# Transposes of the combining weights spread over the experts' stage, the last ten behind its last product; first weight conversions begun two places earlier

## The chip, the core and the metric

The kernel runs on one core of a Trainium2 chip, in one launch. A core has a matrix engine (TensorE, PE in the rows; its weight loads are shown as PEld), a vector engine (VectorE, DVE), a scalar engine (ScalarE, ACT), a general one (GpSimd, POOL) and a queue that issues transfers (SyncE, SP). Each works through its own list of instructions in order, and they wait for each other by semaphores. PE writes its results to a small memory, PSUM, from which ACT or DVE copy them to SBUF, the large on-chip memory. The metric is the device time of one execution in microseconds (us).

## The reference

Three layers follow each other, all in float32. Attention of 8 batches x 8 heads between 512 tokens and 32 state rows, in both directions; a mixture of experts that mixes all 4,608 tokens into 32 slots, runs 8 experts of 4 slots each, and mixes the slots back; and a gated layer over all tokens. Cut to what matters here:

```python
# x: 4608 x 512, phi: 512 x 32, w1: 8 x 512 x 1024, w2: 8 x 1024 x 512
logits = x @ phi
d = softmax(logits, over tokens)
slot_input = (d.T @ x).reshape(8, 4, 512)
for e in range(8):
    slot_out[e] = np.maximum(slot_input[e] @ w1[e], 0.0) @ w2[e]
c = softmax(logits, over slots)            # the combining weights, 4608 x 32
x = c @ slot_out
g = x @ w_gate                             # 512 x 1536
out = (g * sigmoid(g) * (x @ w_val)) @ w_out
```

## The kernel before, in words

The attention comes first (to about 90 us); its order is a written list of short names. Then the experts' stage, and then the last stage, which takes the last 330 us. In the last stage the product with `slot_out` is never made for itself: `slot_out` (the tile `ST`) is multiplied into the gate and value weights once (`fold`, line 842), and the blocks of tokens then multiply their combining weights with these folded weights (line 1169), gate the result and multiply it with the output weights (line 1219).

For that the combining weights must stand transposed, 32 slots by 4,608 tokens, in the tile `cstack`. `c_calc` (line 614) makes them in three generators: `c1` for the first 16 tiles of 128 tokens, `c2` for the next 16 and `c3` for the last 2. Each takes the softmax over slots (DVE, ACT, POOL), splits it into two float16 parts (tile `cc`, on POOL), and then, in groups of eight tiles, has PE transpose them into a PSUM tile (line 628) and ACT copy that to `cstack` (line 629). There are 34 such transposes in five groups: 8, 8, 8, 8 and 2.

The experts run as two groups `g` of four. For a group, `expert_1` takes the first layer's products (line 645), one call step for each of eight 1 MB weight loads; `expert_r` applies scale and ReLU on ACT or DVE (lines 655, 657); `expert_h` transposes the result on PE (line 664) and copies it back (line 666); `expert_2` takes the second layer's products in eight steps `k` (line 676); `expert_o` copies the two halves of the result out of PSUM (`so`, line 692: for group 1 the first half on ACT and the second on DVE), turns them with products against a selection matrix (line 694), and writes or adds them to `ST` (lines 703, 705). After group 1 the last stage starts: ST's maximum is taken (line 973), spread over all rows by a product (line 755), and `fold` multiplies `ST` with the converted weights.

Weights of the last stage arrive as 64-bit numbers whose halves are turned into float32 by `to32` (line 715): one ACT conversion (line 725), then a shift (729), a merge (732) and a second merge (736) on DVE. Before the last stage this is done for two blocks of gate and value weights, `pg` (`prep_w0`), and for the first block of output weights, `pw` (`prep_wo0`). Behind the conversion `pw` takes a maximum (826), spreads it on PE (755), derives a scale on DVE (763 to 829), and writes scaled float16 parts on ACT (833) and DVE (837).

The order of all this is written out by hand: `some(gen, n)` lets a generator take its next n pieces, `run(gen)` all that are left, and every engine gets its instructions in the order in which these calls come. Loads are issued by SP in one list; each waits until its buffer of a ring of 17 is free. `heat(n)` issues n filler products whose result nobody uses.

Of the kernel before, what the change touches and what calls it, by code (L numbers as in the profile page):

```python
# [8 lines left out]
F16 = mybir.dt.float16  # L9
# [20 lines left out]
G0 = 10  # L30
G2 = 0
G1 = 5
CC = 0
NRM = 0, 1
ATD = 1
PA, PB, PC = 0, 0, 0
# [2 lines left out]
HA, HB = 7, 5  # L39
H2 = 0  # L40
H7 = 0
HP_ = 0, 1
LEAD, RATE = 7, 21
CR = 1.0
CN = 2.0
# [39 lines left out]
def attn_moe_glu_kernel(  # L85
# [14 lines left out]
    pe, act, dve, pool = nc.tensor, nc.scalar, nc.vector, nc.gpsimd  # L100
# [31 lines left out]
    def psum(i, shape, dt=F32):  # L132
        return ps[-1].tile(shape, dt, tag=f"p{i}", name=f"p{i}")
# [3 lines left out]
    def psmall(shape, dt=F32):  # L137
        scnt[0] += 1
        i = scnt[0] % (3 - len(ps))
        return ps[-1].tile(shape, dt, tag=f"s{i}", name=f"s{i}")  # L140
# [446 lines left out]
    def heat(n, i=None, src=None):  # L587
        src = ident if src is None else src
        p = pbig([128, 128]) if i is None else psum(i, [128, 128])
        for _ in range(n):  # L590
            pe.matmul(out=p, lhsT=src, rhs=src, start=True, stop=True)
# [17 lines left out]
        (pool, dve)[PA].tensor_tensor(out=dst, in0=dst, in1=bc(r, NSL), op=ALU.mult)  # L609
        yield 1.0  # L610

    CT = []

    def c_calc(t0, n):
        c = wk.tile([128, n, NSL], F32, tag=("sp", "so", "edn")[t0 // 16], bufs=1 + t0 // 32, name="cc")
        yield from slot_softmax(Lg[:, t0:t0 + n, :], n, c)
        cc = wk.tile([128, n, 4, NSL], F16, tag=("stn", "C", "edn")[t0 // 16], bufs=1 + t0 // 32, name="cc16")
        for i in range(2):
            pool.tensor_copy(out=cc[:, :, i, :], in_=c) if i >= PB else act.copy(out=cc[:, :, i, :], in_=c)
        yield 1.0  # L620
        for i in range(2):
            (pool, dve)[i < PC].tensor_tensor(out=cc[:, :, 2 + i, :], in0=c, in1=cc[:, :, i, :], op=ALU.subtract)
        yield 1.0
        for u in range(0, n, 8):
            k = min(8, n - u)
            p = psmall([128, 8, 128], F16)
            for i in range(k):
                pe.transpose(p[:, i, :], cc[:, u + i, :, :].rearrange("p a s -> p (a s)"), CT[1])
            (dve.tensor_copy if (u // 8) % 2 < CC else act.copy)(out=CT[0][:, t0 + u:t0 + u + k, :], in_=p[:, :k, :])
            yield 1.0  # L630

    hT, SO, HP = {}, {}, {}

# [26 lines left out]
    def expert_h(g, i):  # L660
        q = psmall([128, 4, 128])
        h = hS.pop(i)
        for k in range(4):
            pe.transpose(q[:, k, :], h[:, k * 128:(k + 1) * 128], ident)
        t = exq[0][:, 1024 + 512 * i:1536 + 512 * i].rearrange("p (k n) -> p k n", k=4)
        (act.copy, dve.tensor_copy)[i and not g](out=t, in_=q)  # L666
        hT[g, i] = t

    def expert_2(g, lo, hi):
        if lo == 0:  # L670
            SO[g] = [psum(i, [128, 256]) for i in ((2, 0), (2, 1))[g]]
        for k in range(lo, hi):
            for i in range(2):
                u = got.pop(("w2", g, k, i)) if g and k == 7 else got["w2", g, k][:, :, 256 * i:256 * i + 256]
                for j in range(4):
                    pe.matmul(out=SO[g][i][32 * j:32 * j + 32, :], lhsT=hT[g, k // 4][:, k % 4, 32 * j:32 * j + 32],  # L676
                              rhs=u[:, j, :], start=(k == 0), stop=(k == 7))
                if g and k == 7:
                    done()
                    if i == 0:  # L680
                        heat(H7, 0)
            if not (g and k == 7):
                got.pop(("w2", g, k))
                done()
# [12 lines left out]
    def expert_o(g):  # L697
        for i in range(2):
            expert_p(g, i)
            if g:  # L700
                heat(HP_[i], 0)
        if g == 0:
            act.copy(out=ST[:, 0:4, :], in_=OP[g])
        else:
            dve.tensor_tensor(out=ST[:, 0:4, :], in0=OP[g], in1=ST[:, 0:4, :], op=ALU.add)
# [312 lines left out]
    def run(*gens):  # L1018
        for gen in gens:
            for _ in gen:  # L1020
                pass

    def some(gen, n):
        for _ in range(n):
            if next(gen, None) is None:
                return
# [28 lines left out]
    with tc.manual_schedule():  # L1055
# [45 lines left out]
        CT.append(wk.tile([128, 128], F16, tag="gh", name="id16"))  # L1101
        dve.tensor_copy(out=CT[1], in_=ident)
        c1, c2, c3 = c_calc(0, 16), c_calc(16, 16), c_calc(32, 2)
        pw, pg = prep_wo0(), prep_w0()
# [6 lines left out]
        expert_h(0, 0)  # L1111
        expert_r(0, 1)
        some(c2, 4 - C2)
        expert_2(0, 0, 3)
        expert_h(0, 1)
        some(c3, 4)
        expert_2(0, 3, 8)
        some(pg, 10)
        expert_1(1, 0, 1)
        expert_o(0)  # L1120
        warm = sm.tile([128, 1], F32, tag="warm", bufs=1, name="warm")
        act.activation(out=warm, in_=va, func=AF.Silu)
        run(c1)
        expert_1(1, 1, 2)
        run(c2)
        expert_1(1, 2, 4)
        expert_r(1, 0)
        run(c3)
        some(pg, 1)
        expert_1(1, 4, 5)  # L1130
        run(pg)
# [6 lines left out]
        some(pw, 4)  # L1138
        expert_2(1, 0, 3)
        expert_h(1, 1)  # L1140
        expert_2(1, 3, 4)
        run(pw)
        expert_2(1, 4, 8)
        expert_o(1)
        ps1.close()
        ps.append(ctx.enter_context(tc.tile_pool(name="ps2", bufs=1, space=PSUM)))
# [199 lines left out]
```

## Time and profile before

| | us |
|---|---|
| runs before: median (lowest to highest of 3) | 466.17 (465.02 to 468.76) |
| the profiled execution | 466.66 |
| its span, from the first to the last instruction | 464.9 |
| PE busy in the span | 441.1 |
| DVE, ACT, POOL busy | 300.4, 245.8, 180.9 |
| mean granted clock of PE, share of full speed | 0.996 |

The profile is of one execution, by hardware. A row of a timeline merges instructions of one line that follow each other: start, busy time, engine, line, operation, the tile written and the tile read, number of records; in brackets the idle time of the engine just before and who ended it. A float32 product shows as two records. Line numbers are those of the kernel before.

### The profile page before, as it was taken

The numbers are of one execution on the slowest core, as the hardware profiler recorded it, in microseconds if no ns is written. First come the engines' busy times: TensorE is split into PE (matmuls) and PEld (weight loads), VectorE is DVE, ScalarE is ACT, GpSimd is POOL, SyncE is SP. The second block draws the span as 40 slices with busy tenths as digits, with TensorE's granted clock in tenths as the row PEclk, the third lists the DMA queues.
The fourth block names the chain that finished last, engine by engine and source line by source line (L and its number), as shares of the span: only waits on it lengthen the run. The fifth ranks groups of instructions, "written<-read, shape, count | busy, mean of one in ns | idle before, by whom it ended". The sixth has DMA issues, their size and how long they took to land.

```text
span 464.9 us, 9476 instructions
## 1 busy us (share of the span) xinstructions
PE 441.1 (95%) x3723; PEld 244.9 (53%) x3723; DVE 300.4 (65%) x610; ACT 245.8 (53%) x439; POOL 180.9 (39%) x160
## 2 busy tenths in 40 slices
PE   8789998999988999898999999999999999999997
PEld 6477676544453455454555555555555555555553
DVE  3877988467667786968999878544333334345454
ACT  2678877427348797774655644433344433344440
POOL 0113221072017565644756453333333333333331
PEclk9999999999999899999999999999999999999999
DMA  8999999999999203300000000000011112211224
GB/s 313 421 420 413 413 419 419 390 363 421 419 418 421 87 5 126 155 12 1 1 13 0 7 7 1 13 0 1 1 47 45 47 45 57 80 47 45 90 92 180
DMA packets 19436, 75.04 MB, mean 161 GB/s; under 512 B 5440, under 2 KB 6080, under 8 KB 12608
## 3 DMA queue, kind: packets, MB, share of 16 engines
q1 hardware_dynamic: 19392, 74.45, 40.2%
q8 instruction: 29, 0.48, 0.4%
q14 instruction: 15, 0.12, 0.1%
HBM read 64.87 MB, written 8.91 MB: 159 GB/s over the span
## 4 chain that ended last, share of the span: by engine, by line
PE 70%; DMA 9%; DVE 7%; issue 5%; POOL 5%; ACT 3%; SPq 0%; POOLq 0%; DVEq 0%; ACTq 0%
PE p L1219 44%; PE p L1169 7%; DMA u<-in_wgv_dram 4%; DMA u<-in_xn_dram 4%; PE p L676 3%; POOL hl L1183 3%; PE p L645 3%; PE p L270 2%; POOL u L723 2%; PE p L315 2%; DVE osb L1233 1%; PE s L370 1%; DMA stN<-in_stn_dram 1%; PE s L443 1%; DVE sh L1174 1%
## 5 line engine op out<-in xcount | busy, mean ns | idle before, releaser
L1219 PE MATMUL p<-wo,hl 128*128 128x512 f16 x1014 | 238.2, 381 | 1.8 <-DVE osb L1233 1.7
L1183 POOL TENSOR_TENSOR hl<-sh,hl 128x512 f16<-128x512 f32 x102 | 126.4, 1240 | 191.9 <-ACT hl L1182 188.5
L1219 PEld LDWEIGHTS <-hl 128*128 128x128 f16 x1218 | 118.4, 98 | 123.9 <-issue 4.4
L1174 DVE SCALAR_TENSOR_TENSOR sh<-p,segk,sh 128x512 f32<-128x512 f32 x102 | 76.2, 747 | 85.0 <-ACT sh L1170 83.7
L1170 ACT ACTIVATE sh<-p,sg 128x512 f32<-128x512 f32 x85 | 58.4, 687 | 128.6 <-PE p L1169 128.6
L1182 ACT CAST hl<-sh 128x512 f16<-128x512 f32 x102 | 62.4, 612 | 12.7 <-DVE sh L1174 12.6
L1233 DVE SCALAR_TENSOR_TENSOR osb<-p,segm,osb 128x512 f32<-128x512 f32 x67 | 49.9, 746 | 22.4 <-PE p L1219 22.2
L1219 PE MATMUL p<-bqm,hl 128*128 128x512 f16 x204 | 49.6, 379 | 0.0
L1169 PE MATMUL p<-cstack,gvs 128*128 128x256 f16 x272 | 41.5, 274 | 0.8 <-DVE sh L1174 0.5
L1169 PEld LDWEIGHTS <-gvs 128*128 128x128 f16 x272 | 26.7, 99 | 19.2 <-issue 2.2
L357 POOL TENSOR_TENSOR a<-a,r 128x1024 f32<-128x1024 f32 x7 | 13.4, 1915 | 56.3 <-DVE r L353 17.2
L732 DVE SCALAR_TENSOR_TENSOR u<-u 128x512 uint32<-128x512 uint32 (+1 forms) x33 | 26.4, 809 | 13.4 <-POOL u L723 13.2
L723 POOL TENSOR_SCALAR u<-u 128x512 uint32<-128x512 uint8 x30 | 26.5, 884 | 2.5
L1231 ACT ACTIVATE osb<-p,segk 128x512 f32<-128x512 f32 x28 | 19.2, 692 | 5.2 <-PE p L1219 5.2
L1169 PE MATMUL p<-cstack,gv 128*128 128x256 f16 x136 | 20.4, 273 | 0.0
L736 DVE SCALAR_TENSOR_TENSOR gvf<-gvf,u 128x512 uint32<-128x512 uint32 (+1 forms) x22 | 19.9, 913 | 0.2
L315 PE MATMUL p<-cs,atA 128*128 128x128 f32 x128 | 17.9, 277 | 1.8 <-DVE atA L280 0.5
L1169 PEld LDWEIGHTS <-gv 128*128 128x128 f16 x136 | 13.3, 98 | 8.8
L310 ACT ACTIVATE atA<-atA,nm 128x512 f32<-128x512 f32 x16 | 10.7, 718 | 12.1 <-PE p L315 12.1
L315 PEld LDWEIGHTS p<-cs,atA 128*128 128x128 f32 x128 | 14.3, 140 | 3.6 <-DVE atA L280 1.0
L676 PE MATMUL p<-u,exq 128*32 128x256 f32 x256 | 14.8, 380 | 0.7 <-ACT exq L666 0.7
L725 ACT ACTIVATE gvf<-u 128x512 f32<-128x512 f32 (+1 forms) x22 | 14.8, 722 | 0.0
(214 smaller groups left out, 451.3 us busy)
## 6 DMA issues: line engine op xcount, KB each, us to landing
u<-in_w_dram SPq DMA_DIRECT2D x23, 1024.0 KB, 13.8
u<-in_wgv_dram SPq DMA_DIRECT2D x12, 1024.0 KB, 17.4
u<-in_xn_dram SPq DMA_DIRECT2D x8, 1040.0 KB, 17.9
out_dram<-osb SPq DMA_DIRECT2D x15, 512.0 KB, 2.8
early<-in_w_dram SPq DMA_DIRECT2D x14, 512.0 KB, 9.1
u<-in_wo_dram SPq DMA_DIRECT2D x6, 1024.0 KB, 17.8
u<-in_xt_dram SPq DMA_DIRECT2D x3, 1024.0 KB, 7.3
early<-in_w_dram SPq DMA_DIRECT2D x1, 1024.0 KB, 9.8
```

Of the source, the lines that this page charges most:

```text
L315: pe.transpose(p[:, j, q * 128:(q + 1) * 128], stsA[:, q, j * 128:(j + 1) * 128], ident)
L676: pe.matmul(out=SO[g][i][32 * j:32 * j + 32, :], lhsT=hT[g, k // 4][:, k % 4, 32 * j:32 * j + 32], rhs=u[:, j, :], start=(k == 0), stop=(k ...
L723: pool.tensor_scalar(out=lo[:, c], in0=byte[:, c], scalar1=2.0 ** -5, scalar2=-31.0 / 64, op0=ALU.mult, op1=ALU.add)
L732: dve.scalar_tensor_tensor(out=lo[:, c], in0=hi[:, c], scalar=0x80000000, in1=lo[:, c], op0=ALU.bitwise_and, op1=ALU.bitwise_or)
L736: dve.scalar_tensor_tensor(out=tu[:, c], in0=tu[:, c], scalar=3, in1=lo[:, c], op0=ALU.logical_shift_left, op1=ALU.bitwise_or)
L1169: pe.matmul(out=p[v][:, 256 * i:256 * i + 256], lhsT=GV[2 * q + i][v], rhs=rhs, start=True, stop=True)
L1170: act.activation(out=sh[:, 0, :], in_=p[0], func=AF.Silu, scale=sgs[q])
L1174: dve.scalar_tensor_tensor(out=sh[:, 1, :], in0=p[1], scalar=(kap0[0] if k == 0 else seg_scale(*seg)[0][q]), in1=sh[:, 0, :], op0=ALU.mult ...
L1182: act.copy(out=t[:, 0, :], in_=sh[:, 1, :])
L1183: pool.tensor_tensor(out=t[:, 1, :], in0=sh[:, 1, :], in1=t[:, 0, :], op=ALU.subtract)
L1219: pe.matmul(out=accs[x], lhsT=t[:, u // 2, c], rhs=WO[2 * q + j][:, u % 2, :], start=first and u == 0 and j == 0, stop=last and (j, u) == ...
L1233: dve.scalar_tensor_tensor(out=o, in0=accs[i], scalar=rsc, in1=o, op0=ALU.mult, op1=ALU.add)
```

## The change

`c_calc` gives its last part, one group's transposes and copy, to a new function `c_move`, and keeps its `cc` tile where that can find it. The calls are moved:

- the first two groups (of `c1`) go from behind group 0's `expert_o` to places between the steps of its `expert_2`;
- the third group (the first of `c2`) keeps its place;
- the fourth group and the last two transposes go behind the last products of group 1's `expert_o`, in one PSUM tile of the tag `p0`; the one filler product that stood there is gone;
- the first three pieces of `pg` (one ACT conversion, the shift and the first merge on DVE) go ahead of group 0's `expert_2`;
- the rest of `pw` goes from behind step 3 to behind step 5 of group 1's `expert_2`.

```diff
     def c_calc(t0, n):
...
+        CCS[t0] = cc
...
         for u in range(0, n, 8):
-            k = min(8, n - u)
-            p = psmall([128, 8, 128], F16)
-            for i in range(k):
-                pe.transpose(p[:, i, :], cc[:, u + i, :, :].rearrange("p a s -> p (a s)"), CT[1])
-            (dve.tensor_copy if (u // 8) % 2 < CC else act.copy)(out=CT[0][:, t0 + u:t0 + u + k, :], in_=p[:, :k, :])
+            c_move(t0, u, min(8, n - u), psmall([128, 8, 128], F16))
             yield 1.0
+
+    def c_move(t0, u, k, p):
+        for i in range(k):
+            pe.transpose(p[:, i, :], CCS[t0][:, u + i, :, :].rearrange("p a s -> p (a s)"), CT[1])
+        act.copy(out=CT[0][:, t0 + u:t0 + u + k, :], in_=p[:, :k, :])
...
     def expert_o(g):
         for i in range(2):
             expert_p(g, i)
-            if g:
-                heat(HP_[i], 0)
+        if g:
+            p = psum(0, [128, 16, 128], F16)
+            c_move(16, 8, 8, p[:, 0:8, :])
+            c_move(32, 0, 2, p[:, 8:10, :])
...
         some(c2, 4 - C2)
+        some(pg, 3)
         expert_2(0, 0, 3)
         expert_h(0, 1)
+        some(c1, 1)
         some(c3, 4)
-        expert_2(0, 3, 8)
-        some(pg, 10)
+        expert_2(0, 3, 6)
+        some(c1, 1)
+        expert_2(0, 6, 8)
+        some(pg, 7)
         expert_1(1, 0, 1)
         expert_o(0)
...
-        run(c1)
         expert_1(1, 1, 2)
-        run(c2)
+        some(c2, 1)
         expert_1(1, 2, 4)
         expert_r(1, 0)
-        run(c3)
         some(pg, 1)
...
-        expert_2(1, 3, 4)
+        expert_2(1, 3, 6)
         run(pw)
-        expert_2(1, 4, 8)
+        expert_2(1, 6, 8)
         expert_o(1)
```

What this does to the engines' lists is seen at three places. In the changed file the transposes and their copy are lines 629 and 630, the fold is line 849, and other lines of the last stage are two to four higher than before.

The first place is PE's list around the end of the experts' stage (`so`: the copied result, `p_1952`: the PSUM tile of the last transposes, `cc_1605` and `cc_1675`: the parts of `c2` and `c3`, `gvf` and `ST`: the fold's operands). Before:

```order
L694 MATMUL s_1957<-cs,so 128x32 [waits Activation_49]
...
L694 MATMUL s_1957<-cs,so 128x32 [waits DVE_49]
...
L591 MATMUL p_1967<-cs 128x128
L847 MATMUL p_1985<-gvf,ST 32x128 [waits DVE_49,PE_49]
L847 MATMUL p_1985<-gvf,ST 32x128 x7
L755 MATMUL s_1994<-cs,mst 128x128 [waits DVE_49]
```

And in the change, where the pair of rows `cc_1605` stands eight times:

```order
L694 MATMUL s_1943<-cs,so 128x32 [waits Activation_49]
...
L694 MATMUL s_1943<-cs,so 128x32 [waits DVE_49]
...
L629 LDWEIGHTS cc_1605
L629 MATMUL p_1952<-id_1522,cc_1605 128x128
...
L629 LDWEIGHTS cc_1675 [waits Pool_49]
L629 MATMUL p_1952<-id_1522,cc_1675 128x128 [waits Activation_49]
L629 MATMUL p_1952<-id_1522,cc_1675 128x128
L849 MATMUL p_1981<-gvf,ST 32x128 [waits DVE_49,Activation_49]
L849 MATMUL p_1981<-gvf,ST 32x128 x7
L757 MATMUL s_1990<-cs,mst 128x128 [waits DVE_49]
```

The filler is gone, and ten transposes stand between the L694 products and the fold. Two waits for ACT are new: in the built program the ninth transpose waits for the count that ACT reaches with the copy of the first eight, and the fold's first product for the count that it reaches with the copy of the last two.

The second place is ACT's list from the first experts' result on (`gvf` and `wof`: converted weights, `cstack`: the copies of transposes, `so`: copies of results). Before:

```order
L666 COPY exq<-s_1591 128x512 [waits PE_49]
L601 ACTIVATE cc<-cc 128x64 [waits DVE_49]
L725 ACTIVATE gvf<-u 128x1024 [waits DMAHW7_49,DMAHW5_49]
L725 ACTIVATE gvf<-u 128x1024 [waits DMAHW6_49,DMAHW0_49]
L692 COPY so<-p_1610 128x256 [waits PE_49]
L692 COPY so<-p_1611 128x256 [waits PE_49]
```

In the change:

```order
L666 COPY exq<-s_1591 128x512 [waits PE_49]
L727 ACTIVATE gvf<-u 128x1024 [waits DMAHW7_49,DMAHW5_49]
L630 COPY cstack<-s_1653 128x1024 [waits DMAHW5_49,PE_49]
L599 ACTIVATE cc<-cc 128x64 [waits DVE_49]
L630 COPY cstack<-s_1710 128x1024 [waits PE_49]
L727 ACTIVATE gvf<-u 128x1024 [waits DMAHW6_49,DMAHW0_49]
L692 COPY so<-p_1615 128x256 [waits PE_49]
L692 COPY so<-p_1616 128x256 [waits PE_49]
```

The first conversion moved up, and the second now stands behind two copies to `cstack`. On DVE the shift and the first merge of the same weights likewise moved up, from behind the `c3` softmax to ahead of the copy of line 666.

The third place is PE's list in group 1's second layer (`p_1864` and `p_1850`: the first half of the result, `mxw`: the maximum of the output weights). Before:

```order
L676 MATMUL p_1864<-u,exq 32x256 [waits DMAHW5_49]
...
L755 MATMUL s_1904<-cs,mxw 128x128 [waits DVE_49,PE_49]
...
L676 MATMUL p_1864<-u,exq 32x256 [waits DMAHW6_49,Activation_49]
...
L676 MATMUL p_1864<-u,exq 32x256 [waits DMAHW7_49]
...
L676 MATMUL p_1864<-u,exq 32x256 [waits DMAHW0_49]
...
L676 MATMUL p_1864<-u,exq 32x256 [waits DMAHW1_49]
```

In the change (these are the rows that begin a step; the rest of each step is left out in both):

```order
L676 MATMUL p_1850<-u,exq 32x256 [waits DMAHW5_49]
...
L676 MATMUL p_1850<-u,exq 32x256 [waits DMAHW6_49,Activation_49]
...
L676 MATMUL p_1850<-u,exq 32x256 [waits DMAHW7_49]
...
L757 MATMUL s_1906<-cs,mxw 128x128 [waits DVE_49,PE_49]
...
L676 MATMUL p_1850<-u,exq 32x256 [waits DMAHW0_49]
...
L676 MATMUL p_1850<-u,exq 32x256 [waits DMAHW1_49]
```

The product that spreads the maximum moved from behind step 3 to behind step 5, so two steps are left behind it where four were. On ACT and DVE the work that hangs on it (lines 833 and 837 of the kernel before) still stands ahead of the copies `so`.

## Rows read from the trace of the kernel before

**Rows 1.** The page, engines: busy us, share of the span, instructions.

```profile
PE 441.1 (95%) x3723; PEld 244.9 (53%) x3723; DVE 300.4 (65%) x610; ACT 245.8 (53%) x439; POOL 180.9 (39%) x160
```

**Rows 2.** Chain of waits, 107 to 130 us: start us, us, what.

```profile
107.04 1.02 PE s L694 x8
...
112.34 1.85 PE p L645 x16
114.19 0.22 PE s L628 x2
...
115.41 0.64 PE s L755 x4
...
123.66 0.42 PE s L755 x2
124.08 3.20 PE p L676 x56
...
127.74 0.04 issue
127.79 1.09 PE s L694 x8
...
129.34 0.64 PE p L847 x16
```

**Rows 3.** Timeline of PE, 107 to 152 us.

```profile
107.89 1.12 PE L628 MATMUL s<-id,cc 128*128 128x128 f16 x16
...
110.82 0.61 PE L628 MATMUL s<-id,cc 128*128 128x128 f16 x8 [0.81 <-ACT cstack L629]
...
136.19 2.76 PE L1219 MATMUL p<-wo,hl 128*128 128x512 f16 x12
...
151.29 1.34 PE L847 MATMUL s<-gvf,ST 128*32 128x128 f32 x28 [2.25 <-DVE gvf L736]
```

**Rows 4.** Timeline of ACT, 103 to 127 us.

```profile
103.45 2.32 ACT L725 ACTIVATE gvf<-u 128x1024 f32<-128x1024 f32 x2
...
114.91 0.37 ACT L629 COPY cstack<-s 128x256 f16<-128x256 f16 x1
...
125.21 1.34 ACT L833 ACTIVATE wo<-wof,wsc 128x512 f16<-128x512 f32 x2 [1.92 <-DVE wsc L829]
```

**Rows 5.** Groups of ACT's instructions, 107 to 113 us: busy us, mean ns.

```profile
L629 ACT COPY cstack<-s 128x1024 f16<-128x1024 f16 x4 | 3.7, 1018 | 0.0
```

**Rows 6.** Timeline of DVE, 101 to 143 us.

```profile
101.77 0.69 DVE L666 COPY exq<-s 128x512 f32<-128x512 f32 x1 [2.14 <-PE s L664]
...
104.72 0.71 DVE L729 TENSOR_SCALAR u<-u 128x1024 uint32<-128x1024 uint32 x1
105.46 1.23 DVE L732 SCALAR_TENSOR_TENSOR u<-u 128x1024 uint32<-128x1024 uint32 x1
...
125.96 1.42 DVE L837 SCALAR_TENSOR_TENSOR wo<-wof,wsc,wo 128x512 f16<-128x512 f32 x2 [0.79 <-ACT wo L833]
127.74 0.42 DVE L692 COPY so<-p 128x256 f32<-128x256 f32 x1 [0.36 <-PE p L676]
...
142.56 0.69 DVE L732 SCALAR_TENSOR_TENSOR u<-u 128x512 uint32<-128x512 uint32 x1 [1.67 <-POOL u L723]
```

**Rows 7.** SP's issue of the last half-load of `w2`; and its us to landing.

```profile
108.06 0.33 SPq L174 DMA_DIRECT2D u<-in_w_dram  x1
...
u<-in_w_dram SPq DMA_DIRECT2D x1, 512.0 KB, 17.1
```

**Rows 8.** Stretches: us, busy PE, PEld, DVE, ACT, POOL, granted clock, DMA share, GB/s.

```profile
12.50:16.50 4.00, 1.88 (x40) 0.60 (x42) 3.45 (x9) 2.53 (x4) 1.39 (x1) 1.00 1.00 418
108.00:112.00 4.00, 2.88 (x38) 1.81 (x36) 3.84 (x5) 3.88 (x6) 0.47 (x2) 1.00 1.01 420
152.00:156.00 4.00, 4.00 (x23) 1.78 (x23) 2.33 (x4) 2.05 (x5) 2.66 (x3) 0.57 0.38 158
153.00:153.50 0.50, 0.50 (x3) 0.23 (x2) 0.00 (x0) 0.50 (x2) 0.50 (x1) 0.50 0.74 311
```

More of the change, by code (lines that the diff above doesn't have):

```diff
@@ L32 @@
 G1 = 5
-CC = 0
 NRM = 0, 1
@@ L41 @@
 H7 = 0
-HP_ = 0, 1
 LEAD, RATE = 7, 21
@@ L610, in slot_softmax @@
         yield 1.0
-    CT = []
+    CT, CCS = [], {}
     def c_calc(t0, n):
```

## The prediction

> **What bounds the kernel now.** I began with the page: TensorE (PE) is busy nearly all the span [rows 1], so what counts is time in which PE waits or is made to wait. The change touches one stretch, from about 98 to 131 us, where the two groups of four experts are computed and the first weights of the last stage are folded. So the next view is the chain of waits through that stretch [rows 2]. The reader is to see two things. From 108.06 (107.04 + 1.02) to 112.34 the chain goes through the transposes of the combining weights: 4.28 us in which PE does 32 of the 34 transposes and only one block of expert products. And from 123.66 on it runs over PE, ACT and PE again: the last products, the copies of their result, and the fold at 129.34, from which the whole last stage hangs.
>
> The timelines say what happens inside. On PE [rows 3] sixteen transposes take 1.05 us (107.89 to the next start at 108.94), and the third group of eight starts only after 0.81 us of waiting for ACT's copy of an earlier group. On ACT one such copy takes 1.02 us [rows 5]. On DVE [rows 6] the row at 101.77 has 2.14 us of idle time ahead of it, which is where the early conversions go. A load of the second layer's weights lands 17 us after its issue [rows 7]. The granted clock is 1.00 of full speed (2.4 GHz) in the stretch with the transposes [rows 8].
>
> **The change, part by part.**
>
> *Transposes spread.* The first two groups of eight now stand between the first group's second-layer products, before 108.06: they cost what they cost before, 1.05 us, and their copies on ACT have products to hide behind. So the L694 products end at 108.06 + 1.05 = 109.11. Then one block of products (half of the 1.85 us that sixteen take [rows 2], 0.93) and one group of eight (0.53) follow, and the row that began at 112.34 begins at 109.11 + 0.93 + 0.53 = 110.57, 1.77 us sooner. The two transposes at 114.19 (0.22) are gone from there too. PE is 1.99 us ahead at the row of 115.41.
>
> *First conversions begun early.* One ACT conversion, and a shift and a merge on DVE, are moved ahead. On DVE they need 0.71 + 1.23 = 1.94 us [rows 6], and the idle time before the 101.77 copy is 2.14: nothing on the path. If that cover were short (GpSimd works beside it) the copy would be late by at most one merge, 1.23, and PE needs it one group of transposes (0.53) and one step (0.91) after its start: 0 to 0.5 us, I take 0. The second ACT conversion (1.16, half of 2.32 [rows 4]) now stands behind a cstack copy and ahead of the copies that release L694; it ends about 107.6, and PE is in a block of products until 108.1: 0. The buffers of the second-layer weights come free up to 1.05 us later, and SP, whose order is unchanged, issues the next loads later by that; with 17 us between issue and landing the landing times stay. The last half-load, issued at 108.06, lands at 125.2 [rows 7], and its use falls at 125.3: 0, with 0.4 as its bound.
>
> *Scaling of the first output weights (L755, L833, L837) moved two steps back.* Before, L755 stood behind step 3 (counted from 0) of the eight, at 123.66. Now it stands behind step 5: 123.66 - 1.99 + 2 x 0.91 (0.91 is 16/56 of the 3.20 us row) = 123.50. Almost the same time, but PE now has only two steps left behind it: the products end at 123.50 + 0.42 + 1.83 = 125.75. What hangs on L755 takes as long as before: DVE's L837 ended 127.38 - 123.66 = 3.72 us after it [rows 6], so now at 127.22; ACT's L833 ended 2.89 us after it [rows 4], now at 126.39. Both stand ahead of the copies `so` on their engines. So DVE's copy of the second half, which waited 0.36 us for PE before, now waits for DVE's own L837: it runs from 127.25 to 127.67, and after a hand-over of 0.04 [rows 2] the second half of L694 (half of 1.09) ends at 128.26. Before it ended at 128.88. Of 1.99 us, 0.62 are left; 1.4 us became a wait for ACT and DVE.
>
> *The last ten transposes.* They follow L694 directly. The filler that stood there lay beside DVE's addition, so its removal gives nothing. If only PE counted, the ten would cost 0.61 + 0.22 and the fold would begin at 129.1. But the order with its waits shows more: the ninth transpose waits for ACT's copy of the first eight, out of the same tile; and the fold waits for ACT's copy of the last two. That makes a round trip: eight transposes (0.61) to 128.87, ACT's copy (1.02) to 129.93, two transposes (0.22) to 130.19, ACT's copy (0.37) to 130.60, fold at 130.64, each with a hand-over of 0.04. Queued behind the waiting fold on PE are L755 for ST's maximum and the second half of the fold, and for these wait ACT's `gt` and the scale of everything after.
>
> *Sum.* 130.64 - 129.34 = **+1.30 us** at the start of the last stage. That stage is tied to its own start (its first conversion on DVE, at 142.56, waits for POOL and for no load [rows 6]), so the difference stays. The profiled execution took 466.66 us; one like it takes 467.96. The median of the runs shown lies 0.49 below the profiled one: **467.5 us**. Bounds of the sum: from +0.8 (copies that overlap with the drain of the transposes, PE's start 0.4 better) to +2.2 (late DVE copy and late half-load together).
>
> *A rule against the change.* [Rows 8] show 108 to 112, with 32 transposes in it, at a granted clock of 1.00, 2.4 GHz. The Trainium skill (TensorE: Matmul & The Clock Gate, Part 4: PE-mode transpose) says that transposes do not count as activity of PE for its clock in the way products do. By that rule the ten transposes hold the clock less than the removed filler did, and the time would be that of rival 2. The row does not bear it out, and does not refute it, as products stood around the transposes.
>
> **Rivals.**
>
> 1. *The fold does not wait for the copies*: they are done in time, or the waits are for something long past. Then the fold starts at 129.1, 0.25 us earlier than before: 465.9 us, not slower. It decides from the point where both copies are through when DVE has added ST. For it: ACT has nothing else to do then. Against: a copy's own 1.02 us, which no idle ACT makes shorter. Chance 0.15.
>
> 2. *The clock falls.* PE sat idle for 2.25 us until 151.29 [rows 3], and from 152 to 156 the mean granted clock was 0.57, with 0.50, which is 1.2 GHz, inside [rows 8]. By the sum above PE is idle about 1.1, 0.4, 1.1 and 0.4 us between 125.75 and 130.64, with 1.9 us of short work between. A fall would slow the fold and what follows it. The fall of 152 to 156 cost 0.43 x 4 = 1.7 us; here some of the work is ACT's and DVE's, so I put it at 1.5 (an estimate from that row). Against: in 12.5 to 16.5 PE was busy for no more than 1.88 us and the clock stayed at 1.00. 1.3 + 1.5 = 2.8: 469.0 us. Chance 0.17.
>
> 3. *The later fall goes away.* If the shift by 1.3 us spares the stretch at 152 to 156, PE gets 1.7 us back: 1.3 - 1.7 = -0.4, 465.8 us. For it: the fall stands behind one idle time of PE, and where that lies in the span moves. Against: nothing in the change works on it, and its own length stays. Chance 0.10.
>
> 4. *The scaling chain is no wait*, because L755 runs sooner. Then the fold starts up to 1.4 us earlier than in my sum, and the spread pays for the round trip: 466.1. It would need L755 at 122.1; PE's place in its own queue sets it (the chain goes through PE there). Chance 0.05.
>
> **How the numbers follow.** Forecast 0.53, rivals 0.15, 0.17, 0.10, 0.05. The likeliest case gives 467.5, with its own bounds 467.0 to 468.4. The range takes in the rivals on both sides: 465.4 to 469.5. One per cent, about what a measurement of this kernel can tell from no change, is 4.7 us; no case reaches it alone. Faster by over 1% would need rivals 3 and 4 and more: 0.03. Slower by over 1% needs a fall of the clock that lasts longer than the one seen: 0.06. The rest, 0.91, is within 1%.
>
> **What would show it.** Right: PE's second half of the L694 products waits for DVE's `so` copy behind L837; the last two transposes wait about 1 us for ACT's cstack copy; the fold waits for the second one; the first L1219 row starts 1.3 us later than at 136.19 [rows 3]; no stall of PE at the remaining transposes near 110. Wrong: a fold that starts before 129.5, a first L1219 row before 136.0, a granted clock below 1.00 between 126 and 136, or a new wait of PE between 98 and 108 for DVE's copy or for a load.

## The result, and the profile after

| | before | after |
|---|---|---|
| median of the runs | 467.65 us (11 runs, 465.02 to 469.46) | 470.62 us (11 runs, 468.74 to 472.38) |
| profiled execution, span | 466.66, 464.9 us | 470.62, 468.9 us |

The change makes the kernel slower: ratio 1.0067, 95% interval 1.0039 to 1.0096, which is 3.0 us by the medians. That lies within one per cent, as forecast, but above the range: 467.5 was predicted, and 465.4 to 469.5 were given.

The part of the program ahead of the experts' stage is the same in all kernels here, and its length differs from one profiled execution to the next: the first L645 product of the stage starts between 89.9 and 92.2 us. So in all that follows, places are counted from that product, 90.01 us before and 91.36 after. The difference of the two is 1.35.

Here is PE in the changed kernel, from the scaling's L757 (L755 before) to the first product of the output weights, L1223 (L1219 before). Each line has the start, the duration (both us), engine and line, operation and tiles, shape and count; in brackets the idle time ahead of it and what ended that.

```profile
124.71 0.49 PE L757 MATMUL s<-cs,mxw 128*128 128x128 f32 x2
125.13 1.99 PE L676 MATMUL p<-u,exq 128*32 128x256 f32 x32
127.97 0.63 PE L694 MATMUL s<-cs,so 128*128 128x32 f32 x4 [0.84 <-ACT so L692]
128.88 0.63 PE L694 MATMUL s<-cs,so 128*128 128x32 f32 x4 [0.28 <-DVE so L692]
129.35 0.61 PE L629 MATMUL p<-id,cc 128*128 128x128 f16 x8
131.06 0.27 PE L629 MATMUL p<-id,cc 128*128 128x128 f16 x2 [1.10 <-ACT cstack L630]
131.79 1.08 PE L849 MATMUL p<-gvf,ST 128*32 128x128 f32 x16 [0.46 <-ACT cstack L630]
...
140.50 0.82 PE L1223 MATMUL p<-wo,hl 128*128 128x512 f16 x3
```

First the four waits: 0.84, 0.28, 1.10 and 0.46 us, 2.68 us in all. In the kernel before, PE had a single one on its way to the fold:

```profile
129.34 0.64 PE L847 MATMUL p<-gvf,ST 128*32 128x128 f32 x16 [0.17 <-DVE ST L705]
```

Less 1.35, the fold starts at 130.44 on the scale of before: 1.10 us later than at 129.34, against 1.30 in the sum. Then the fold's own duration: its sixteen products take 1.08 us and not the 0.64 of [rows 2]. And then the last line: 140.50 - 1.35 = 139.15, 2.96 us later than the 136.19 of [rows 3]. So 1.86 us more are lost between the fold and the first product of the output weights.

Why that is, the granted clock tells. This is a table of stretches of the changed kernel, with the columns of [rows 8]; the clock is the third number from the end.

```profile
108.00:112.00 4.00, 4.00 (x48) 1.97 (x36) 3.84 (x4) 2.91 (x5) 1.09 (x5) 1.00 1.02 422
128.00:132.00 4.00, 2.16 (x22) 1.75 (x26) 1.44 (x4) 1.39 (x2) 0.00 (x0) 0.93 1.01 420
131.50:132.00 0.50, 0.21 (x4) 0.20 (x8) 0.00 (x0) 0.24 (x1) 0.00 (x0) 0.50 1.10 459
132.00:136.00 4.00, 3.57 (x43) 2.23 (x36) 1.48 (x7) 0.34 (x2) 0.00 (x0) 0.50 1.01 416
137.50:138.00 0.50, 0.50 (x4) 0.38 (x4) 0.45 (x2) 0.00 (x0) 0.00 (x0) 0.50 1.02 426
138.50:139.00 0.50, 0.26 (x3) 0.09 (x1) 0.00 (x0) 0.50 (x2) 0.00 (x0) 1.00 1.02 426
```

Through the last waits ahead of the fold the clock goes from 1.00 to 0.50, which is 1.2 GHz, and it is back at 1.00, 2.4 GHz, by 138.5. That is the fall that rival 2 described. The first line answers to the second of [rows 8]: with the transposes spread, PE is busy for all of the 4 us where it was for 2.88. These are the products that stand at 115.41 in [rows 2], before and after:

```profile
115.34 0.71 PE L755 MATMUL s<-cs,mg 128*128 128x128 f32 x4
114.73 0.71 PE L757 MATMUL s<-cs,mg 128*128 128x128 f32 x4
```

Less 1.35 they come 1.96 us sooner, where the prediction had 1.99. What the spread was to give, it gave.

The fall is not a matter of the one profiled execution: the mean granted clock of the whole execution was 0.980 to 0.989 in all eleven runs of the changed kernel, and of the 88 runs of the kernel before that were taken beside the experiments, three are at 0.989 and the others at 0.991 to 1.000.

From the first L1223 row to the end it is 468.9 - 140.50 = 328.4 us; before, 464.9 - 136.19 = 328.7. Nothing was given back later.

### The profile page after: what moved, and what is told of

Read it like the earlier page. It is cut to its first block, busy times and chain, and to the rows that moved or that the text cites. A ratio compares the mean times of both kernels' runs of the same rounds, so it can differ in the third digit from the quotient of the medians.

```text
span 468.9 us, 9470 instructions
## 1 busy us (share of the span) xinstructions
PE 443.7 (95%) x3721; PEld 246.7 (53%) x3721; DVE 300.9 (64%) x610; ACT 245.9 (52%) x439; POOL 180.4 (38%) x160
## 4 chain that ended last, share of the span: by engine, by line
PE 70%; DVE 8%; POOL 7%; issue 6%; DMA 5%; ACT 3%; SPq 0%; POOLq 0%; DVEq 0%; ACTq 0%
PE p L1223 44%; PE p L1173 7%; POOL hl L1187 4%; DMA u<-in_xn_dram 4%; PE p L645 3%; POOL u L725 3%; PE p L676 3%; PE p L268 2%; PE p L313 2%; DVE osb L1237 1%; DMA stN<-in_stn_dram 1%; PE s L368 1%; DVE sh L1178 1%; PE p L248 1%; PE s L441 1%
## 5 line engine op out<-in xcount | busy, mean ns | idle before, releaser
L1223 PE MATMUL p<-wo,hl 128*128 128x512 f16 x1014 | 237.6, 380 | 1.8 <-DVE osb L1237 1.7
L1223 PEld LDWEIGHTS <-hl 128*128 128x128 f16 x1218 | 118.4, 98 | 123.7 <-issue 4.5
L1223 PE MATMUL p<-bqm,hl 128*128 128x512 f16 x204 | 49.6, 379 | 0.0
```

The lines of the kernel that those rows point to most:

```text
L1223: pe.matmul(out=accs[x], lhsT=t[:, u // 2, c], rhs=WO[2 * q + j][:, u % 2, :], start=first and u == 0 and j == 0, stop=last and (j, u) == ...
```

## The experiments

My theory after the result: the change adds two separate waits, the scaling chain ahead of the copies `so` and the round trip of the last ten transposes, which make 1.1 us less what the spread saves; and the idle time that they bring to PE makes the clock fall, for another 1.9 us. The rivals: the clock falls because a filler was taken out, because transposes stand where products stood, or because the idle time comes in several pieces; or the early conversions cost something. Medians are of 5 rounds beside the kernel before on the same chip, which took 467.30 us in the first two groups of four kernels and 466.92 in the last of three.

**The scaling at its old place** (the round trip alone):

```diff
-        expert_2(1, 3, 6)
+        expert_2(1, 3, 4)
         run(pw)
-        expert_2(1, 6, 8)
+        expert_2(1, 4, 8)
```

> The change with one part undone: the scaling of the first output weights stands behind step 3 again, the rest is as in the change. Theory (the +3.0 us of the change are 1.1 us of round trip through ACT at the fold and 1.9 us of a clock that falls because PE idles four times between 127 and 132 us): the two idle times ahead of the L694 products (0.84 and 0.28) go, the fold comes about 1.1 us sooner. If the two of the round trip alone (1.10 and 0.46) don't bring the clock down, it stays at 1.00 up to 140 and the kernel is level with before (-0.3 to +0.5 us); if they do, it is +1.9 us. Rival (the scaling hides under its own cover anyway): no change against the change, +3.0 us.

Measured: 468.84 us (467.71 to 471.87), ratio 1.0042 [1.0019, 1.0065]. Here is PE from the last transposes on, and the clock.

```profile
128.66 0.27 PE L629 MATMUL p<-id,cc 128*128 128x128 f16 x2 [1.10 <-ACT cstack L630]
129.39 1.08 PE L849 MATMUL p<-gvf,ST 128*32 128x128 f32 x16 [0.46 <-ACT cstack L630]
...
138.10 2.76 PE L1223 MATMUL p<-wo,hl 128*128 128x512 f16 x12
```

```profile
130.00:132.00 2.00, 2.00 (x30) 1.11 (x21) 0.61 (x3) 0.00 (x0) 0.00 (x0) 0.50 0.98 406
132.00:134.00 2.00, 1.57 (x15) 1.14 (x12) 0.95 (x5) 0.74 (x3) 0.00 (x0) 0.50 1.04 426
```

No wait for the scaling is left, and the fold starts 39.18 us behind the first expert product (129.39 - 90.21), 1.25 sooner than in the changed kernel: the scaling's place costs 1.25 there. But the clock falls all the same, with 1.10 and 0.46 us of idle time, which is the second of the two outcomes that I had given, and the first L1223 row comes 1.71 us later than before (47.89 against 46.18). In eleven of the twelve runs the mean clock of the execution is 0.982 to 0.989.

**The last ten transposes at their old place, and the filler** (the scaling's wait alone):

```diff
         for i in range(2):
             expert_p(g, i)
-        if g:
-            p = psum(0, [128, 16, 128], F16)
-            c_move(16, 8, 8, p[:, 0:8, :])
-            c_move(32, 0, 2, p[:, 8:10, :])
+            if g:
+                heat(i, 0)
...
-        some(c2, 1)
+        run(c2)
...
+        run(c3)
```

> The change with one part undone: the last ten transposes and the filler stand where they stood before, the spread of the first sixteen, the early conversions and the scaling behind step 5 stay. Theory: no round trip, so the fold follows the addition to ST as before; PE has 0.75 us more ahead of the scaling, its idle times ahead of L694 stay (0.84 and 0.28), the clock stays at 1.00; level with before, -0.3 to +0.5 us. Rival (the spread or the early conversions cost the time): +2 us or more stays.

Measured: 468.69 us (467.49 to 470.87), ratio 1.0030 [1.0011, 1.0050]. In the profile the fold is level with before (39.43 against 39.33), as expected. That the clock would hold was a miss: it fell between 130 and 132. PE's timeline there, and the clock:

```profile
129.60 0.63 PE L694 MATMUL s<-cs,so 128*128 128x32 f32 x4 [0.90 <-ACT so L692]
130.52 0.63 PE L694 MATMUL s<-cs,so 128*128 128x32 f32 x4 [0.28 <-DVE so L692]
130.98 0.47 PE L589 MATMUL p<-cs 128*128 128x128 f32 x2
131.62 1.08 PE L847 MATMUL p<-gvf,ST 128*32 128x128 f32 x16 [0.17 <-DVE ST L705]
```

```profile
130.00:132.00 2.00, 1.54 (x17) 1.27 (x20) 1.08 (x4) 0.00 (x0) 0.00 (x0) 0.85 1.07 442
```

No transpose stands in these lines, and the filler (L589) does, and still the fold takes 1.08 us. So neither the transposes nor the missing filler are needed for the fall. Each of the two waits can bring it by itself. The scaling's does not do so every time: the mean clock of the execution is 0.985 to 0.989 in seven of the twelve runs, 0.993 in three and 0.996 in two, and none of the changed kernel's eleven is above 0.989.

**Fillers in the gaps** (all waits stay, PE works in them):

```diff
+        if g:
+            heat(3, 0)
         for i in range(2):
             expert_p(g, i)
+            if g and i == 0:
+                heat(1, 0)
         if g:
             p = psum(0, [128, 16, 128], F16)
             c_move(16, 8, 8, p[:, 0:8, :])
+            heat(4, 1)
             c_move(32, 0, 2, p[:, 8:10, :])
+            heat(2, 1)
```

> The change with ten filler products on PE in its four idle times: three ahead of the L694 products, one between their halves, four between the eighth and the ninth transpose, two ahead of the fold. They feed nothing. Theory: the chain through ACT keeps its length, the clock stays at 1.00 between 126 and 140 us; 1.9 us faster than the change, +1.1 us against before. Rival (the clock's fall costs nothing, as ACT and DVE set the time there): as the change, +3.0 us.

Measured: 468.20 us (466.45 to 468.89), ratio 1.0023 [1.0005, 1.0041]. PE's timeline from the last second-layer products on (L589 are the fillers, L855 is the fold):

```profile
126.31 0.64 PE L676 MATMUL p<-u,exq 128*32 128x256 f32 x8 [0.62 <-DMA u<-in_w_dram]
126.88 0.94 PE L589 MATMUL p<-cs 128*128 128x128 f32 x6
...
129.14 1.11 PE L589 MATMUL p<-cs 128*128 128x128 f32 x8
130.40 0.27 PE L629 MATMUL p<-id,cc 128*128 128x128 f16 x2 [0.15 <-ACT cstack L630]
130.51 0.66 PE L589 MATMUL p<-cs 128*128 128x128 f32 x4
131.28 0.64 PE L855 MATMUL p<-gvf,ST 128*32 128x128 f32 x16
```

The fold is no earlier: it starts 40.87 us behind the first expert product, 0.44 later than in the changed kernel. In this execution PE waits 0.62 us for a load ahead of the last second-layer products, and the first three fillers stand behind these, so the L694 products come later; what the fillers cost without that wait is not shown. But the fold takes 0.64 us, the granted clock is 1.00 throughout 126 to 140, and from the fold to the first product of the output weights it is 6.85 us (138.13 - 131.28) in place of 8.71 (140.50 - 131.79). Before it was 6.85 too (136.19 - 129.34). That is the price of the fall: 1.86 us, and work without any use on PE gets it back. The mean clock of the execution is 0.993 to 1.000 in all twelve runs.

**Two PSUM tiles for the last ten, and products in place of transposes.** First the two waits of the round trip are joined, then only the kind of instruction is changed:

```diff
-            p = psum(0, [128, 16, 128], F16)
-            c_move(16, 8, 8, p[:, 0:8, :])
-            c_move(32, 0, 2, p[:, 8:10, :])
+            c_move(16, 8, 8, psum(0, [128, 8, 128], F16))
+            c_move(32, 0, 2, psum(1, [128, 2, 128], F16))
```

> The changed kernel, but the last ten transposes write two PSUM tiles, eight into one and two into another, so that the ninth no longer waits for ACT's copy of the first eight; the scaling stays behind step 5. Theory (TensorE's idle time ahead of the fold makes the granted clock fall, and costs 1.9 us): the 1.10 us wait ahead of the last two transposes goes, they stand directly behind the eight, and one wait of 1.2 to 1.6 us for both copies now stands ahead of the fold, which starts 0.2 us sooner relative to the first expert product than in the changed kernel (130.2 instead of 130.44 on the scale of before). Idle time in all is hardly less, so the clock still falls to half for some 7 us: 469.5 to 470.6 us, ratio 1.005 to 1.007. Rival A (waiting in several pieces is what matters, one piece is harmless): the clock holds at 1.00 from 126 to 140, 468.3 us, ratio 1.002.

```diff
+    def c_prod(t0, u, k, p):
+        for i in range(k):
+            pe.matmul(out=p[:, i, :], lhsT=CCS[t0][:, u + i, :, :].rearrange("p a s -> p (a s)"), rhs=CT[1], start=True, stop=True)
+        act.copy(out=CT[0][:, t0 + u:t0 + u + k, :], in_=p[:, :k, :])
...
-            p = psum(0, [128, 16, 128], F16)
-            c_move(16, 8, 8, p[:, 0:8, :])
-            c_move(32, 0, 2, p[:, 8:10, :])
+            p = psum(0, [128, 8, 128])
+            c_prod(16, 8, 8, p)
+            p = psum(1, [128, 2, 128])
+            c_prod(32, 0, 2, p)
```

> The same as the kernel with two PSUM tiles, but the last ten are ordinary products of the weights' halves with the f16 identity into f32 tiles, not PE-mode transposes; order, sizes and waits are the same. Theory (idle time brings the fall, whatever the instruction beside it is): a fall of the same length at the same place as with two tiles and transposes, the two kernels within 0.5 us of each other. Rival B (transposes do not hold the clock as products do, the rule of the Trainium skill, TensorE: Matmul & The Clock Gate, Part 4: PE-mode transpose): with products the clock stays at 1.00 from 126 to 140, the first product of the output weights comes 1.9 us sooner than with transposes, 468.3 us, ratio 1.002.

Measured: 470.38 us (468.67 to 470.84), ratio 1.0062 [1.0038, 1.0086] with two tiles; 469.74 us (469.21 to 470.88), ratio 1.0055 [1.0035, 1.0075] with products. The lines are PE's with two tiles, then PE's with products.

```profile
127.59 0.64 PE L676 MATMUL p<-u,exq 128*32 128x256 f32 x8 [0.52 <-DMA u<-in_w_dram]
128.40 0.63 PE L694 MATMUL s<-cs,so 128*128 128x32 f32 x4 [0.17 <-ACT so L692]
129.32 0.63 PE L694 MATMUL s<-cs,so 128*128 128x32 f32 x4 [0.28 <-DVE so L692]
129.78 0.72 PE L629 MATMUL p<-id,cc 128*128 128x128 f16 x10
131.77 1.08 PE L848 MATMUL p<-gvf,ST 128*32 128x128 f32 x16 [1.26 <-ACT cstack L630]
```

```profile
130.12 0.72 PE L634 MATMUL p<-id,cc 128*128 128x128 f16 x10
132.11 1.08 PE L855 MATMUL p<-gvf,ST 128*32 128x128 f32 x16 [1.27 <-ACT cstack L635]
```

All ten now run in one piece, and of the round trip one wait is left, ahead of the fold. The fold starts 0.45 us sooner (39.98 behind the first expert product), but the fall is there all the same, and longer: at 138 to 140 the granted clock is still 0.50, and the first product of the output weights comes at 49.16, where the changed kernel had 49.14. With products it comes at 49.14, and the fall has the same length. The medians lie 0.64 us apart, a little more than expected, with intervals that overlap. So joining the two waits does not spare the fall, and the kind of instruction does not show. Rival A is not tried by these two runs, as PE's idle time still comes in four pieces: 0.52 us for a load, 0.17, 0.28 and 1.26 with two tiles, and 0.40, 0.29, 0.28 and 1.27 with products. What speaks against it is the later stall below, where a single piece of 2.25 us stands ahead of a fall in half of the profiled executions. The Trainium skill (TensorE: Matmul & The Clock Gate, Part 4: PE-mode transpose) says that transposes do not count as busy time of PE for the clock in the way products do; no run here confirms that, and it is not the cause here.

**The removed filler put back** behind the L694 products of the changed kernel (`heat(i, 0)` in the loop, nothing else):

> The changed kernel with the filler behind the second L694 products put back ahead of the ten transposes; nothing else. Theory (the idle time of the waits brings the fall, not the missing filler of 0.47 us): the clock still falls to half between 131 and 138 and the time is that of the changed kernel plus 0 to 0.4 us: 470.5 us, ratio 1.007. Rival E (the filler was what held the clock): the clock stays at 1.00, 468.6 us, ratio 1.003.

Measured: 469.63 us (468.96 to 471.42, 6 runs), ratio 1.0085 [1.0057, 1.0114]; that of the changed kernel was 1.0067, and the intervals overlap. The clock was 0.75 at 128 to 132 and 0.50 from there to 140. The filler did not hold it.

**The early conversions alone**, in the kernel before:

```diff
         some(c2, 4 - C2)
+        some(pg, 3)
         expert_2(0, 0, 3)
...
-        some(pg, 10)
+        some(pg, 7)
```

> The kernel before with one part of the change alone: one ACT conversion, a shift and a merge on DVE are begun two places ahead. Theory (they lie in DVE's idle time): no wait of PE between 98 and 108 for DVE's copy at 101.8, fold 39.3 us behind the first expert product as before, 467.3 us, ratio 0.999 to 1.001. Rival C (DVE's merge, slower beside GpSimd, makes the copy late): PE waits 0.3 to 0.5 us there, 467.8 us, ratio 1.001.

Measured: 467.47 us (465.41 to 468.98), ratio 1.0001 [0.9979, 1.0023]: nothing that the time can show. The profile shows more, in the timelines of DVE and then of PE:

```profile
101.34 1.95 DVE L732 SCALAR_TENSOR_TENSOR u<-u 128x1024 uint32<-128x1024 uint32 x1
103.22 0.68 DVE L666 COPY exq<-s 128x512 f32<-128x512 f32 x1
```

```profile
103.95 3.66 PE L676 MATMUL p<-u,exq 128*32 128x256 f32 x64 [0.15 <-DVE exq L666]
```

The merge takes 1.95 us where [rows 6] had 1.23, DVE's copy is late, PE waits 0.15 us for it, and the L645 products behind these come 0.36 us later than before (16.35 behind the first expert product; 15.99): rival C's place and size, and a miss of my theory. In the changed kernel the merge takes 1.95 us as well, but eight transposes stand ahead of the products that need the copy, and no wait of PE is seen there. So there the term is 0, as I took it.

**The spread without a tail.** The last point is a kernel that keeps what worked. The third group of transposes stays where the change has it, the fourth stands between second-layer products of the second group, the last two behind the scaling at its old place, and the filler is back (the lines that take the ten from the tail and put the filler back are those shown for the ten at their old place):

```diff
...
-        expert_2(1, 0, 3)
+        expert_2(1, 0, 2)
+        run(c2)
+        expert_2(1, 2, 3)
         expert_h(1, 1)
-        expert_2(1, 3, 6)
+        expert_2(1, 3, 4)
         run(pw)
-        expert_2(1, 6, 8)
+        run(c3)
+        expert_2(1, 4, 8)
```

> A version with the spread but without the two costs: first sixteen transposes and early conversions as in the change, third group as in the change, fourth group between steps 1 and 2 of group 1's second layer, the last two behind the scaling, which stands behind step 3 again; the filler is back. Theory: PE loses the waits of 0.81 and 0.31 us at the third and fourth group of before, and gains no new one; -0.7 to -1.3 us against before, clock 1.00 between 100 and 140. Rival (spreading wins nothing, since PE's place is set by ACT or DVE elsewhere): level with before.

Measured: 465.71 us (464.51 to 468.56), ratio 0.9963 [0.9942, 0.9984]: faster than before. The fold starts 38.18 us behind the first expert product, 1.15 sooner than before, with the clock at 1.00 from 100 to 140. With it the places of the fold add up: the spread gives 1.15 us in this kernel, the round trip costs 1.00 (39.18 against 38.18), the scaling's new place 1.25 (39.43 against 38.18), and -1.15 + 1.00 + 1.25 is the +1.10 of the changed kernel.

**The later stall filled.** Around 150 PE waits 2.24 to 2.29 us in a later part of the fold for DVE's `gvf` in every profiled execution so far, and in some executions the clock falls behind it [rows 3, 8]. Filler products were put into that wait, 14, then 9, and 9 in the kernel before (`stall` is set for that part of the fold alone):

```diff
...
             for k in range(4):
+                if stall and kc == 0 and k == 2:
+                    for _ in range(9):
+                        pe.matmul(out=p[64:128, :], lhsT=ident[:, 0:64], rhs=ident, start=True, stop=True)
                 pe.matmul(out=p[32 * k:32 * k + 32, :], ...
```

> The version with spread transposes, nothing behind the last product and the scaling at its old place, which took 465.71 us; added are 14 filler products of 128x128 in the fold at 150 to 152, between its first two products and the next, where PE waited 2.25 us for DVE's gvf. Theory (that idle time makes the granted clock fall at 152 to 156 in part of the executions, 1.7 us each time): the wait becomes 0.3 us, the clock stays at 1.00 from 150 to 158, no time is added, and the median comes down by 0.3 to 1.7 us: 464.0 to 465.4, ratio 0.993 to 0.996. Rival D (the last stage is limited by DVE, ACT and POOL for some us behind it and takes the loss back): no change, 465.7 us, ratio 0.9965.

> The version with spread transposes and the filled stall, with 9 filler products in place of 14: the 14 took 3.27 us where the wait is 2.25, so the second half of the fold came late by some 0.8 us. Theory: 9 take 2.1 us, nothing is late, the clock stays at 1.00 from 150 to 158 in every execution, and from the first product of the output weights to the end it is always the shorter of the two times seen, 327.1 us and not 328.5: 464.3 us, ratio 0.994. Rival: the executions without a fall were the rule there already, and the fillers bring nothing: 465.0 to 465.7, ratio 0.996.

> The kernel before with one edit alone: the 9 filler products in the fold at 150, where PE waited 2.25 us ahead of the fall of the clock at 152 to 156. Theory: that idle time brings the later fall, in many executions of the kernel before; with the fillers the clock is 1.00 from 150 to 158 and the time from the first product of the output weights to the end is 327.1 us in place of 328.7: 466.0 us, ratio 0.997. Rival: the fall comes from something else, and the ratio is 1.000.

Measured: 465.04 us (464.59 to 466.73), ratio 0.9960 [0.9939, 0.9980] with 14; **464.24 us** (463.77 to 465.31), ratio 0.9947 [0.9927, 0.9967] with 9; 465.89 us (465.19 to 467.51), ratio 0.9995 [0.9978, 1.0012] with 9 in the kernel before. Fourteen were too many: they took 3.27 us, and the fold's second half came late. With nine, PE's timeline at the place (L849 the fillers, L850 the fold):

```profile
147.72 2.18 PE L849 MATMUL s<-cs 128*64 128x128 f32 x18
150.08 1.23 PE L850 MATMUL s<-gvf,ST 128*32 128x128 f32 x28 [0.18 <-DVE gvf L736]
```

In the two profiles with nine the clock is 1.00 from 148 to 160. The version with spread transposes and nine fillers beats both kernels. How much of that the fillers give is open: its interval overlaps that of the spread alone, and in the kernel before the same edit gave no ratio that differs from 1, where I had expected 0.997, though the medians lie 1.0 us apart (465.89 and 466.92).

The places of all the profiled executions, in us:

| kernel | fold, behind the first expert product | first product of the output weights | from there to the end |
|---|---|---|---|
| before | 39.33 | 46.18 | 328.7 |
| after | 40.43 | 49.14 | 328.4 |
| scaling at its old place | 39.18 | 47.89 | 328.4 |
| ten in place | 39.43 | 48.14 | 328.5 |
| fillers in the gaps | 40.87 | 47.72 | 328.7 |
| two tiles; products | 39.98; 39.98 | 49.16; 49.14 | 327.1; 327.0 |
| filler back | 41.06 | 50.33 | 327.1 |
| early conversions alone | 39.69 | 46.54 | 327.1 |
| spread, no tail | 38.18 | 45.04 | 327.1 |
| the same, 14; 9 fillers | 38.18; 38.18 | 45.03; 45.03 | 327.8; 327.1 |
| before with 9 fillers | 39.33 | 46.18 | 327.0 |

## Why the prediction was wrong

**The sum was right, nearly step by step.** In the numbers of before (1.35 taken off), L757 starts at 123.36 (123.50 predicted), the products end at 125.77 (125.75), the second half of L694 ends at 128.16 (128.26), the fold starts at 130.44 (130.64). ACT's and DVE's rows show the two waits as they were drawn: the copy `so` of the first half queued behind the scaling's L835, that of the second half behind L839, and the two copies of `cstack`, 1.01 and 0.37 us.

```profile
126.32 1.33 ACT L835 ACTIVATE wo<-wof,wsc 128x512 f16<-128x512 f32 x2 [3.65 <-DVE wsc L831]
127.56 0.35 ACT L692 COPY so<-p 128x256 f32<-128x256 f32 x1
129.99 1.01 ACT L630 COPY cstack<-p 128x1024 f16<-128x1024 f16 x1 [2.08 <-PE p L629]
131.37 0.37 ACT L630 COPY cstack<-p 128x256 f16<-128x256 f16 x1 [0.36 <-PE p L629]
```

```profile
127.08 1.41 DVE L839 SCALAR_TENSOR_TENSOR wo<-wof,wsc,wo 128x512 f16<-128x512 f32 x2 [0.79 <-ACT wo L835]
128.41 0.41 DVE L692 COPY so<-p 128x256 f32<-128x256 f32 x1
```

Rival 1 (the fold does not wait) is out by the 0.46 us ahead of it. Rival 4 is out by the 0.84 and 0.28. Of the signs of being right, the three waits of PE came and no stall near 110 did, but the first row of the output weights came 2.96 us later and not 1.3. Of the signs of being wrong one came, the clock below 1.00 between 126 and 136.

The late half-load was nothing in the changed kernel, as taken. In three kernels made from it, though, PE waited 0.62, 0.52 and 0.40 us for a load ahead of the last second-layer products, the first two beyond the bound of 0.4. With two tiles and with products this lay inside the wait for `so`: the first L694 products start 36.61 us behind the first expert product there, as in the changed kernel.

**The step that failed is the clock of PE: the sum has no term for its fall, which was given as rival 2 with a chance of 0.17, and it cost 1.86 us.** I had its mechanism and its idle times: about 1.1, 0.4, 1.1 and 0.4 us were foretold, 0.84, 0.28, 1.10 and 0.46 came. I held it unlikely because of one row: in 12.5 to 16.5 PE was busy for 1.88 of 4 us and the clock stayed at 1.00 [rows 8]. In 128 to 132 of the changed kernel PE was busy for 2.16 of 4 us, more, and it fell. The busy time of a stretch does not tell the two apart, and one row in which nothing happened was weak evidence. That it was luck the later traces show. Here is the end of that same place in the attention, before and with the scaling at its old place, PE and then the clock:

```profile
16.38 0.99 PE L370 MATMUL s<-u,e 128*32 128x65 f32 x51 [0.88 <-issue]
16.69 1.73 PE L368 MATMUL s<-u,e 128*32 128x65 f32 x51 [0.92 <-issue]
```

```profile
16.00:20.00 4.00, 3.34 (x71) 2.99 (x72) 2.59 (x10) 1.68 (x3) 1.02 (x1) 1.00 1.01 424
16.00:20.00 4.00, 3.31 (x60) 3.14 (x61) 1.82 (x8) 0.00 (x0) 1.28 (x1) 0.57 1.02 428
```

The idle time is nearly the same, but in the second execution the clock falls behind it and the same products take 1.73 us in place of 0.99. It does so in five of the thirteen profiled executions. The row that I should have weighed higher is the one with the fall: 2.25 us of idle time ahead of 152 to 156, against 2.68 us in four pieces here.

**Its price was also too low**: 1.5 us by my estimate, 1.86 by the fillers' run. With it the sum is 1.10 + 1.86 = 2.96 us, which is the difference of the medians, 2.97. That the two agree so closely is in part luck, as the interval of the ratio leaves room for 1.8 to 4.5 us.

**The base was 0.8 to 1.5 us too low.** I built on the median of the three runs shown, 466.17; over 11 runs it is 467.65, 467.30 over the 31 to 35 beside the first eight experiments, and 466.92 over the 22 beside the last three. The 3.1 us between 467.47, the prediction before rounding, and 470.62 are 1.48 of base and 1.86 of clock, less 0.20 by which the sum was too high. With the base of 11 runs the range would have reached to 471.0 and held the result, so that the range failed is owed to the base as well; that the change costs 2.96 us and not 1.30 is owed to the clock.

The table says what a part of that spread is. From the first product of the output weights to the end it is either 327.0 to 327.1 us or 328.4 to 328.7 (327.8 only where 14 fillers overshoot). The upper value goes with a granted clock below 1.00 behind the stall at 150 to 152, the lower with 1.00 there, in all of them. That fall comes in five of the ten profiled executions in which the stall is unfilled, whatever the kernel, and costs about 1.5 us; why it comes in one and not in the next is not shown. Another part lies ahead of the experts' stage, whose first product starts at 89.9 to 92.2 us; what moves it was not tried. Rival 3 made a property of the change out of what differs from execution to execution.

**The early conversions** cost nothing in the changed kernel, as predicted, though for another reason than DVE's spare time: the transposes moved ahead cover a copy that is late.

## What to carry to other kernels

Work that is moved from a crowded place to the end of a chain is paid for in waits there, and each wait of TensorE is paid twice where it brings the clock down: once by its length, once by the slower work behind it. So spread such work between products that need nothing from it, keep the last hand-overs free of round trips through another engine, and look at the granted clock behind every place where the sum adds idle time; a wait that can't be removed may be worth a few filler products, but no more than fit into it: ahead of the fold they won back 1.86 us, in the later stall a gain by them alone is not shown. And take the base from many runs before a difference of a few tenths of a per cent is argued.

## What the runs showed of the hardware

- Idle time as short as 1.10 and 0.46 us, with 0.27 us of work between, brought the granted clock from 1.00 to 0.50 (the scaling at its old place); 2.25 us in one piece did so in only five of ten executions, and 0.92 and 0.73 to 1.05 us in the attention in five of thirteen, by which the same idle time may or may not bring a fall.
- The clock stayed at 0.50 for some 7 us, 131.5 to 138 in the changed kernel, though PE was busy for 3.57 of 4 us from 132 on. This cost 1.86 us; PE's rows there still wait for ACT (0.43 and 0.30 us), so not all of the chain is PE's. In the kernels with two tiles, with products and with the filler back the clock stayed at 0.50 for some 10 us, and from the fold to the first product of the output weights it took 2.3 to 2.4 us longer than before.
- A merge on DVE of 128x1024 words took 1.23 us at one place and 1.95 two places ahead. GpSimd works beside it at both places, and its own conversion of 128x512 took 1.17 us before and 2.04 beside the slow merge; what makes them slow was not tried.
